# Transposing q, k and the attention output with the DMA crossbar instead of TensorE, in batches 3 to 7

## The chip, the cores and the metric

The kernel runs on one core of one Trainium2 chip. The metric is device time in microseconds (us); each kernel was run several times, and medians are quoted. The engines are called as the profile calls them: PE is TensorE (PEld its weight loads), DVE is VectorE, ACT is ScalarE, POOL is GpSimd, SP is SyncE. SP and POOL compute little here; POOL issues the loads, SP issues the stores and, after the change, the crossbar transposes. L508 in a profile line is line 508 of the kernel that the profile belongs to. In the rows of 40 digits each digit is the busy share of one of 40 equal slices of the span, in tenths (9 is 90% or more); PEclk is the clock granted to PE, in tenths of full speed. The line that begins with the shares of PE, DMA and so on ("PE 73%; DMA 10%") splits up the chain of waits that ended last. Of the tile names, duo and uno are PSUM tiles, the crossbar turns cb into qx and xb into xt, dl is the shift, xk and xr are the blends, rl and kk the mix before and after squaring, rs the sigmoid, ot the output.

## The reference

Eight batches of sliding-window attention with a linear position bias, then a channel mix, on 576 positions with 8 heads of 64.

```python
# attention: q, k, v are (8, 8, 576, 64)
scores = scale * np.matmul(q, k.transpose(0, 1, 3, 2))
mask = (rel >= 0) & (rel < 128)
scores = np.where(mask, scores + bias[None], -1000000000.0)
attn = softmax(scores)                      # written out in the reference
x = (attn @ v)                              # then heads side by side: (8, 576, 512)

# channel mix
x_prev = shift of x by one position, zeros first
xk = mu_k * x + (1.0 - mu_k) * x_prev
xr = mu_r * x + (1.0 - mu_r) * x_prev
k = np.maximum(xk @ w_k, 0.0)               # 512 -> 1024
v = k * k @ w_v                             # 1024 -> 512
r = 1.0 / (1.0 + np.exp(-(xr @ w_r)))
return r * v
```

Two transposes per batch follow from this. The scores need q and k with the head dimension on the partitions, while they are loaded with positions there. The mix needs the attention output with the model dimension on the partitions, while attention delivers it by positions.

## The kernel before

The kernel plans its own order. Each piece of work is a node with an engine, an assumed duration and latency, and a priority; a list scheduler written in Python plays the plan through once, at build time, and the order that it finds is the order in which every engine executes. On the chip the engines keep to this order: an instruction whose data are late holds up everything behind it on the same engine (a wait of 6.06 us is followed below). That matters for the whole argument.

```python
def rank(prio):                        # attention: due by its group, ahead of the mix by A
    ...
        return {e: ((k - A[e]) * 4.87,) + tuple(prio) for e in A}
...
A = {PE: 9.0, ACT: 7.0, DVE: 7.0, VIR: 0}
...
def full_load(b, i, h, g):             # q or k of one batch: 4 loads by POOL
    src = (q, k)[i][b, :, 0:SM].rearrange("h (p r) d -> p h r d", p=128)
    return [dma(POOL, 256, issue_t(1024), lambda e, r=r: nc.gpsimd.dma_start(
        out=cb_buf[h.idx][:, i, r], in_=src[:, :, r]), [g]) for r in range(NF)]
...
for g in range(G):                     # four groups of two heads in each batch
    ...
    def emit_t(e, g=g, hp=hp, hc=hc):
        for n in range(2 * NF):        # eight 128x128 transposes of q and k on PE
            nc.tensor.transpose(
                one(hp).bitcast(BF16)[:, 128 * n:128 * n + 128],
                cb_buf[hc.idx][:, n // NF, n % NF, 2 * g:2 * g + 2].rearrange(
                    "p h d -> p (h d)"), ident)
    t = op(PE, 0.0565 * 8, cl[b] + paced(b, g), prio + (3,), emit_t, [hp, hq], [hc])
    y = op(ACT, act_t(1024), [t], ...)             # copy out of PSUM
    _, (m0, m1) = scores(b, g, ...)
    r, hx = attend(b, g, 0, NJ, ha, [m0, m1] + vl[b], prio)   # PE, then DVE normalizes
    a, c = out_t(b, g, 0, NJ, hx, [r], prio, xh[P], xth[b])   # 5 PE transposes, ACT copy,
                                                              # DVE shift and two blends
...
# channel_mix ends each block of 128 rows with a store by SP, out of one of three buffers
y = plan.add(SPE, 0.6, 0.0, [d], (1, len(plan.nodes)),
             lambda e, ho=ho, row=row: nc.sync.dma_start(
    out=of[row:row + 128, :], in_=ot_buf[ho.idx]))
```

The softmax here doesn't subtract the row's maximum and nothing guards it: scores larger than these inputs give would overflow.

## Time and profile before

| | before |
|---|---|
| time, median of 4 runs | 254.72 us (253.82 to 255.14) |
| span of the profiled execution | 252.6 us |
| span less PE's busy time | 252.6 - 233.2 = 19.4 us |
| loads land within the first | about 161 us |

### The profile page before, as it was taken

What the parts mean: (1) busy time and instruction counts of PE and PEld (TensorE: products, weight loads), DVE (VectorE), ACT (ScalarE), POOL (GpSimd) and SP (SyncE); (2) the same over time, 40 slices, a digit from 0 to 9 for tenths busy, and PEclk for the clock granted to TensorE, in tenths of its full rate; (3) what the DMA queues carried; (4) which work ended last, traced back from release to release, by engine and by line L of the source; (5) the groups of instructions that cost most, each with busy time, mean ns of one, the idle gap of its engine ahead of it and who ended that gap; (6) DMA issues with size and microseconds to landing.
All of it is one profiled execution on the core that took longest, in us unless ns stands there. A gap on an engine that the chain in (4) does not pass through costs nothing.

```text
span 252.6 us, 5776 instructions
## 1 busy us (share of the span) xinstructions
PE 233.2 (92%) x2259; PEld 143.9 (57%) x2288; DVE 195.0 (77%) x433; ACT 175.3 (69%) x285; POOL 104.7 (41%) x130
## 2 busy tenths in 40 slices
PE   2979985989989999999999999999999999999993
PEld 1436764565655766556565775565666754445461
DVE  7676776789998999979995997897798887325242
ACT  3486889388896887888497795975896755426250
POOL 8959894899966580509540576000000000000000
PEclk9999999999999999999999999999999999999999
DMA  8999999999998997909991599902101202031112
GB/s 110 151 169 162 156 146 177 152 190 156 203 154 63 169 166 81 134 2 107 188 157 42 76 169 120 91 0 86 66 20 43 86 0 84 3 125 42 65 62 84
DMA packets 119916, 26.87 MB, mean 106 GB/s; under 512 B 112208, under 2 KB 114768, under 8 KB 119888
## 3 DMA queue, kind: packets, MB, share of 16 engines
q0 software_dynamic: 112560, 16.52, 95.2%
q1 hardware_dynamic: 7328, 9.97, 11.5%
q8 instruction: 18, 0.29, 0.5%
q14 instruction: 10, 0.08, 0.1%
HBM read 33.56 MB, written 9.44 MB: 170 GB/s over the span
## 4 chain that ended last, share of the span: by engine, by line
PE 73%; DMA 10%; DVE 5%; ACT 4%; issue 4%; POOL 2%; DVEq 0%; POOLq 0%; ACTq 0%
PE uno L628 23%; PE uno L661 21%; PE uno L647 10%; PE duo L485 5%; PE duo L525 5%; DMA wv_sb<-in_moe_w_v_dram 4%; PE uno L554 3%; PE uno L781 3%; ACT at L496 2%; DMA cb<-in_k_dram 2%; DMA ts<-in_k_dram 2%; PE duo L472 2%; POOL cb L365 2%; DMA out_dram<-ot 1%; PE uno L724 1%
## 5 line engine op out<-in xcount | busy, mean ns | idle before, releaser
L628 PE MATMUL uno<-xk,wk_sb 128*128 128x256 bf16 (+2 forms) x411 | 72.4, 318 | 1.1 <-DVE xk L573 0.8
L661 PE MATMUL uno<-wv_sb,kk 128*128 128x512 bf16 x280 | 70.5, 379 | 3.1 <-DMA wv_sb<-in_moe_w_v_dram 1.3
L496 ACT ACTIVATE at<-duo 128x1024 bf16<-128x1024 f32 (+2 forms) x68 | 65.5, 994 | 7.1 <-PE duo L485 6.8
L635 ACT ACTIVATE rl<-uno 128x256 bf16<-128x256 f32 (+2 forms) x104 | 47.8, 480 | 29.8 <-PE uno L628 26.9
L628 PEld LDWEIGHTS <-wk_sb 128*128 128x128 bf16 x416 | 39.1, 99 | 21.8 <-issue 1.3
L639 DVE TENSOR_TENSOR kk<-rl 128x256 bf16<-128x256 bf16 (+2 forms) x104 | 33.1, 338 | 13.1 <-ACT rl L635 11.8
L661 PEld LDWEIGHTS <-kk 128*128 128x128 bf16 x288 | 25.9, 98 | 28.2 <-DMA wv_sb<-in_moe_w_v_dram 1.4
L502 DVE TENSOR_TENSOR at<-at,mask 128x1024 bf16<-128x1024 bf16 x56 | 37.2, 684 | 4.9 <-ACT at L496 4.9
L672 DVE SCALAR_TENSOR_TENSOR ot<-rs,uno 128x512 f32<-128x512 bf16 x36 | 24.6, 683 | 18.3 <-PE uno L661 14.8
L455 ACT COPY qk<-uno 128x1024 bf16<-128x1024 bf16 (+1 forms) x30 | 30.1, 1004 | 10.3 <-PE uno L781 9.0
L344 POOL DMA_DIRECT2D vs<-in_v_dram x32 | 28.5, 902 | 19.8 <-PE duo L525 16.4
L647 PE MATMUL uno<-wr_sb,xr 128*128 128x512 bf16 x128 | 35.1, 379 | 0.9 <-issue 0.2
L365 POOL DMA_DIRECT2D cb<-in_q_dram x28 | 24.7, 904 | 24.8 <-PE uno L781 24.8
L654 ACT ACTIVATE rs<-uno 128x512 bf16<-128x512 f32 x36 | 22.0, 611 | 16.5 <-PE uno L647 14.2
L573 DVE SCALAR_TENSOR_TENSOR xk<-dl,muk_sb,xt 128x576 bf16<-128x576 bf16 (+2 forms) x36 | 26.9, 747 | 0.5
L365 POOL DMA_DIRECT2D cb<-in_k_dram x28 | 24.8, 914 | 6.0 <-DMA wv_sb<-in_moe_w_v_dram 4.2
L573 DVE SCALAR_TENSOR_TENSOR xr<-dl,mur_sb,xt 128x576 bf16<-128x576 bf16 (+2 forms) x36 | 26.8, 744 | 0.0
L525 PEld LDWEIGHTS <-at 128*128 128x128 bf16 x576 | 22.1, 99 | 6.9 <-ACT at L496 1.9
L455 ACT COPY xt<-uno 128x576 bf16<-128x576 bf16 (+2 forms) x36 | 21.2, 589 | 5.6 <-PE uno L554 4.8
L532 DVE TENSOR_TENSOR xu<-duo,rc 128x640 bf16<-128x640 f32 x28 | 23.1, 824 | 1.0
L647 PEld LDWEIGHTS <-xr 128*128 128x128 bf16 x144 | 13.7, 98 | 14.0 <-issue 0.2
L485 PE MATMUL duo<-qk 64*128 64x256 bf16 (+1 forms) x264 | 20.2, 262 | 1.2 <-DVE xu L532 1.2
(52 smaller groups left out, 215.1 us busy)
## 6 DMA issues: line engine op xcount, KB each, us to landing
out_dram<-ot SPq DMA_DIRECT2D x36, 256.0 KB, 2.1
vs<-in_v_dram POOLq DMA_DIRECT2D x32, 128.0 KB, 5.5
cb<-in_q_dram POOLq DMA_DIRECT2D x28, 128.0 KB, 6.4
cb<-in_k_dram POOLq DMA_DIRECT2D x28, 128.0 KB, 6.0
wk_sb<-in_moe_w_k_dram POOLq DMA_DIRECT2D x1, 1024.0 KB, 9.0
wv_sb<-in_moe_w_v_dram POOLq DMA_DIRECT2D x1, 1024.0 KB, 11.2
ts<-in_q_dram POOLq DMA_DIRECT2D x8, 64.0 KB, 5.7
ts<-in_k_dram POOLq DMA_DIRECT2D x8, 64.0 KB, 5.5
```

Source lines behind the costliest of these rows:

```text
L365: return [dma(POOL, 256, issue_t(1024), lambda e, r=r: nc.gpsimd.dma_start(out=cb_buf[h.idx][:, i, r], in_=src[:, :, r]), [g]) for r in ra ...
L455: (nc.scalar.copy if e == ACT else nc.vector.tensor_copy)(out=out, in_=in_)
L485: nc.tensor.matmul(sa[:, hl, c0:c0 + n], lhsT=kk_, rhs=qq_, start=not bias, stop=True, skip_group_check=True)
L496: lambda e, ah=ah, w=w, hp=hp: nc.scalar.activation(out=ah(), in_=two(hp)[:, :, 0:w], func=AF.Exp, scale=float(scale)), (), [hp])
L502: prio + (2,), lambda e, ah=ah, m0=m0, w=w: nc.vector.tensor_tensor(out=ah(), in0=ah(), in1=mask[:, 2 * g:2 * g + 2, m0:m0 + w], op=ALU.mu ...
L525: nc.tensor.matmul(a[:, hl, t - t0], lhsT=at[:, lo:lo + 128], rhs=vs[:, u, 2 * g + hl, :] if u < NF else tvb[:, 2 * g + hl], start=(u == u ...
L573: lambda e, buf=buf, mu=mu: nc.vector.scalar_tensor_tensor(out=buf[hk.idx][:, g, e0 + c0:e0 + c1], in0=dl_buf[hd.idx][:, 0:n], scalar=mu[: ...
L628: nc.tensor.matmul(one(hp)[:, 0:n], lhsT=wk_sb[:, po, 128 * fo:128 * fo + 128], rhs=xk_buf[hx.idx][:, po, c0:c1], start=(po == 0), stop=(p ...
L635: a = op(ACT, act_t(n), [s], pr, lambda e, hp=hp, hr=hr: nc.scalar.activation(out=rl_buf[hr.idx][:, 0:n], in_=one(hp)[:, 0:n], func=AF.Rel ...
L639: lambda e, fo=fo, hr=hr: nc.vector.tensor_tensor(out=kk_buf[hk.idx][:, fo, 0:n], in0=rl_buf[hr.idx][:, 0:n], in1=rl_buf[hr.idx][:, 0:n], ...
L647: nc.tensor.matmul(one(hp), lhsT=xr_buf[hx.idx][:, po, 128 * c:128 * c + 128], rhs=wr_sb[:, po], start=(po == 0), stop=(po == NPO - 1))
L661: nc.tensor.matmul(one(hv), lhsT=kk_buf[hk.idx][:, fo, o:o + 128], rhs=wv_sb[:, fo], start=(fo == 0), stop=(fo == NFO - 1))
```

## The change

The intent is to take transposes off PE, the busiest engine. From batch 3 on, one crossbar transpose turns a 128x512 block of q or k (all heads at once, eight per batch), straight from SBUF into SBUF, and five turn the attention output of a batch. PE's transposes and ACT's copies out of PSUM disappear there. The normalization may go to ACT or DVE, from batch 1 on. The shift and the two blends move to the end of each batch, and are ranked XD = 4 groups later. One PSUM buffer moves to the pool that mix and transposes now share, and the sigmoid buffers go from 6 to 4. Each load of q or k for these batches now brings 128 consecutive positions instead of every fourth one.

```diff
+    XB = range(3, B)          # batches whose q and k are turned by the crossbar
+    XO = range(3, B)          # batches whose attention output is
+    XD = 4
+    def XU(b, g):             # engines allowed for the normalization
+        return (ACT, DVE) if b else (DVE,)
...
+    qx_buf = many(2, [128, 2, G, SM], BF16, "qx")
+    xb_buf = many(2, [128, NJ, H, D], BF16, "xb")
-    rs_buf = many(6, [128, DM], BF16, "rs")
+    rs_buf = many(4, [128, DM], BF16, "rs")
-    N1 = 3
+    N1 = 4
+    PT = "p1"
...
+    def flip(b, i, j, g):     # one of eight for q and k of a batch
+        return dma(SPE, 190, 1.25, lambda e: nc.sync.dma_start_transpose(
+            out=qx_buf[xbh[b].idx][:, i, :, 128 * j:128 * j + 128],
+            in_=cb_buf[ch[b].idx][:, i, j].rearrange("p h d -> p (h d)")),
+            [g, (cl[b][NF * i + j], 6.0)], (), [ch[b]])
...
+            for t in range(nt):                       # normalization on ACT
+                for hl in range(2):
+                    nc.scalar.activation(out=out_[:, hl, t], in_=a5()[:, hl, t, 0:D],
+                                         func=AF.Copy, scale=rc[:, hl, t:t + 1])
...
+    def out_flip(b, rs, hx, ht):                      # five for the output of a batch
+        for t in range(NJ):
+            rows = min(128, S - 128 * t)
+            n = plan.add(SPE, 1.25 * rows / 128, 0.0, rs + [virt_xt[b]], ...
+                         nc.sync.dma_start_transpose(
+                out=xt_buf[ht.idx][:, :, X0 + 128 * t:X0 + 128 * t + rows],
+                in_=xb_buf[hx.idx][0:rows, t].rearrange("p h d -> p (h d)")))
+            res.append(plan.add(FAB, 0.6 * rows / 128, 0.9, [(n, 1.0)], ...))
...
+        if b in XO:
+            fl = out_flip(b, rs, xbh_o[b], xth[b])
+            for g in range(G):
+                xks[b, g], xrs[b, g] = shift(b, g, 0, S, fl, (0, b, 0, g + XD), xh[P], xth[b])
```

(Cut to its core; "..." marks the cuts, and comments are added.)

## The prediction

> **What bounds the kernel now.** I read three views of the profile in this order: the page of the execution (shares, slices, chain of waits), the busy time of each engine in stretches of the span, and the timeline of PE around single attention groups.
>
> ```profile
> PE 233.2 (92%) x2259; PEld 143.9 (57%) x2288; DVE 195.0 (77%) x433; ACT 175.3 (69%) x285; POOL 104.7 (41%) x130
> PE   2979985989989999999999999999999999999993
> DVE  7676776789998999979995997897798887325242
> ACT  3486889388896887888497795975896755426250
> DMA  8999999999998997909991599902101202031112
> PE 73%; DMA 10%; DVE 5%; ACT 4%; issue 4%; POOL 2%; DVEq 0%; POOLq 0%; ACTq 0%
> 75.00:210.00 135.00, 132.50 (x1361) 83.74 (x1380) 118.43 (x240) 103.31 (x162) 41.95 (x50) 1.00 0.86 90
> 210.00:248.50 38.50, 38.19 (x198) 19.45 (x200) 16.24 (x37) 16.85 (x33) 0.00 (x0) 1.00 0.15 57
> ```
>
> The last two lines give the stretch, its length, then busy us of PE, PEld, DVE, ACT and POOL (with instruction counts), the granted clock, the DMA share and GB/s. There are three stages. Up to about 75 us, PE has gaps and the chain of waits runs through loads: batches 1 to 3 come in as fast as the DMA brings them. From 75 to 210 us PE is busy 132.5 of 135 us, and attention (which runs ahead) and the channel mix share it. DVE is the runner-up at 118.43/135 = 88%, ACT has 77%. From 210 us on there is channel mix alone, PE at 99%, all others under half. So PE sets the end, and DVE stands close behind it in exactly the stage that the change touches. The granted clock is 1.00 throughout.
>
> **What the Trainium skill says.** (1) "Trainium Kernel Development and Optimization", Performance Expectations, calls matmul busy time a bad metric, because matmuls are pipelined. This trace agrees: eight transposes of q and k show 0.61 us and 219 ns each, so they start (0.61 - 0.22)/7 = 56 ns apart.
>
> ```profile
> 162.49 0.61 PE L781 MATMUL uno<-ident,cb 128*128 128x128 bf16 x8
> 162.94 1.89 PE L628 MATMUL uno<-xk,wk_sb 128*128 128x512 bf16 x8
> 164.66 0.44 PE L554 MATMUL uno<-ident,xu 128*128 128x128 bf16 x5
> 164.94 0.62 PE L525 MATMUL duo<-vs,at 128*128 128x65 bf16 x15
> ```
>
> Columns: start, us, engine, line, operation, count. The next matmul starts 0.45 us after the first of the eight, and 0.28 us after the first of the five transposes of the attention output. Those start-to-start times, not 0.61 and 0.44, are what a removal gives back on a full PE. (2) "VectorE: DVE Perf Modes", The three transpose paths: a 128x128 bf16 transpose takes 390 ns on TensorE and 1309 ns through the DMA crossbar, which leaves SBUF in SBUF while TensorE's lands in PSUM. The trace has 219 ns for TensorE, not 390, and no crossbar transpose yet; the PSUM copies it saves are in the trace. (3) "DMA: Bandwidth & Descriptors", Latency and other measured facts, gives 261 GB/s for a DMA transpose: as an estimate from that, 131 KB (128x512 bf16) is 0.50 us of all DMA engines. No run shows it yet. (4) The same page, Queues, rings and completion order: each DMA engine takes turns between queue rows packet by packet, so transposes from SP share with the loads from POOL. The output stores, which share in the same way, land in 2.1 us by the page, so that is tolerable today.
>
> **The change part by part**, for the 5 batches 3 to 7, 4 groups each, 20 groups.
>
> Removed from PE: per group 8 transposes of q and k and 5 of the output, 0.45 + 0.28 = 0.73 us; times 20 = **14.6 us** of PE issue. By busy time it would be 20 x (0.61 + 0.44) = 21 us, but the pipeline tails in that lie under the next matmul, so I do not count them.
>
> Removed from ACT: one copy of 128x1024 and one of 128x576 per group.
>
> ```profile
> L455 ACT COPY qk<-uno 128x1024 bf16<-128x1024 bf16 x28 | 29.0, 1034 | 9.2 <-PE uno L781 9.0
> L455 ACT COPY xt<-uno 128x576 bf16<-128x576 bf16 x28 | 18.0, 643 | 4.6 <-PE uno L554 4.6
> L532 DVE TENSOR_TENSOR xu<-duo,rc 128x640 bf16<-128x640 f32 x28 | 23.1, 824 | 1.0
> L654 ACT ACTIVATE rs<-uno 128x512 bf16<-128x512 f32 x36 | 22.0, 611 | 16.5 <-PE uno L647 14.2
> L496 ACT ACTIVATE at<-duo 128x1024 bf16<-128x1024 f32 x56 | 56.7, 1049 | 1.0 <-PE duo L485 0.9
> ```
>
> That is 20 x (1.03 + 0.64) = 33 us off ACT, all in the middle stage, none of it on the path by itself.
>
> Moved: the normalization (824 ns on DVE) may now go to ACT as ten 128x64 activations. The two ACT rows of 512 and 1024 columns give (1049 - 611)/512 = 0.86 ns a column and a fixed 170 ns, so one takes about 225 ns alone, and perhaps 100 to 200 ns in a row since neighbours overlap: an estimate of 1 to 2 us a group. If half of the 20 groups go there, DVE loses 10 x 0.82 = 8 us and ACT gains about 15. ACT ends near 103 - 33 + 15 = 85 us. The reciprocal, the shift and the two blends stay on DVE, but after the last group of a batch, as one burst of about 4 x (0.45 + 0.81 + 0.81) = 8.3 us.
>
> Does DVE hold the gain back? If the middle stage shrinks by 14.6 us to about 120 us, DVE has 118.4 - 8.2 = 110 us to do in it: 92%. With no move it would be 98%. So the move is what makes the gain possible, and at 92% I expect a little to be lost to queueing: 2 us.
>
> Added: 8 crossbar transposes per batch for q and k and 5 for the output, 65 in all, on SP's queue. The trace shows 21 groups of attention between 75 and 210 us, 6.4 us a group, 26 us a batch. The planner inside the kernel assumes 1.25 us of SP per transpose; taking that as the author's measurement, a batch costs 12.5 x 1.25 = 16 us of SP (the last output piece is half), inside the 23 us a batch has afterwards. The DMA share shows that transfers leave room after 100 us. Attention's result is needed late: by the last two stretches, mix goes on 40 us after attention has ended, so 8 us more from attention to mix is hidden. Loads have room as well: q and k now pass through two load buffers and two transposed ones, which is deeper than before.
>
> One place is exposed: batch 3. Its k loads land near 64 us and the first PE transposes wait for them, one buffer at a time:
>
> ```profile
> 63.51 0.55 PE L781 MATMUL uno<-ident,cb 128*128 128x128 bf16 x7
> 64.32 0.23 PE L781 MATMUL uno<-ident,cb 128*128 128x128 bf16 x1 [0.26 <-DMA cb<-in_k_dram]
> ```
>
> Now all eight crossbar transposes must land first, some 3 to 5 us after the last load (an estimate: two issues and a landing like that of the stores). PE has mix work meanwhile, so I count 1 us. In exchange, PE loses some small waits on ACT's copies and the mix gets a fourth PSUM bank: minus 0.5 us.
>
> **Sum**: 254.9 - 14.6 + 2 + 1 - 0.5 = 242.8; I say 243.0 us, 4.7% faster.
>
> **The rivals.** (a) *The crossbar becomes the bound.* The budget is about 23 us for 13 transposes, so about 1.8 us each. If one occupies the queue for 2.5 us, a batch needs 31 us, more than today's 26, and the kernel is slower, 258 to 275 us. For it: the 1309 ns for a quarter of such a transfer, and DMA slices at 9 up to 100 us. Against it: the 261 GB/s and the author's 1.25 us. (b) *DVE takes over* in the middle stage: if ACT gets few of the normalizations or the bursts collide with the squares for the mix, DVE runs at 98% and the gain halves, about 248 us. For it: DVE's row of nines today. (c) *SP's order turns into a wait*: SP runs in order, and a transpose that waits for a late load holds back the output stores behind it; three output buffers then stop DVE and PE. SP today only waits for outputs, so this is new; it could eat 3 to 10 us, giving 246 to 252. (d) *The gain is larger*, since PE today loses about 9% of the middle stage to small stalls that partly come from transposes waiting for ACT and DVE: at best the 21 us of busy time, 234 us.
>
> **Range and chances.** (b), (c) and a mild (a) pull up and (d) pulls down, so the range is lopsided: 235.0 to 253.0. The 2% line for faster is 249.8. I give (a) in full 0.12, (c) or (a) eating nearly all of the gain 0.15, the rest is faster: 0.73.
>
> **What would show it.** PE busy should fall to about 213 us, with no rows of transposes after batch 2 and the matmul counts 260 lower; ACT busy to about 157 us; the row of the normalization on DVE to about half its count; attention steps of about 5.7 us a group; PE still at nines to the end and still over 70% of the chain of waits. Issue to landing of the crossbar transposes should be 2 to 4 us. I am wrong if transposes or waits of SP stand in the chain, if DVE is at 97% between 75 and 200 us with gaps on PE beside it, if the stores land later and outputs wait for them, or if the tail of pure mix is longer than today's 40 us.

## More of the kernel before

The queue lines give packets, MB, and the time that the packets took as a share of 16 DMA engines over the whole span; the issue lines give count, KB each and the median us from issue to landing.

```profile
q0 software_dynamic: 112560, 16.52, 95.2%
q1 hardware_dynamic: 7328, 9.97, 11.5%
...
out_dram<-ot SPq DMA_DIRECT2D x36, 256.0 KB, 2.1
...
cb<-in_q_dram POOLq DMA_DIRECT2D x28, 128.0 KB, 6.4
```

Queue q0 holds POOL's loads, q1 what SP issues. The 95.2% are a share of the whole span, but the loads are over after some 161 us of it. While they run, their packets therefore take 95.2% x 252.6 / 161 = 149% of the engines' time: on average more than one packet is outstanding on every engine. This is time outstanding, not time occupied: the loads come in bursts. Counted from the packets of the trace between 60 and 160 us, none at all is in flight for 21.9 of the 100 us. That is the room that there is.

## The result, and the profile after

The changed kernel took 267.01 us, median of 4 runs (266.41 to 267.3), against 254.72: a ratio of 1.0485, interval 1.0451 to 1.0518. It is slower. All ratios here are the mean time of one kernel's fast runs over that of the other's fast runs of the same rounds, so they are not quite the ratio of the quoted medians.

From the page of the changed kernel: busy times, three rows of slices, the DMA queues and the chain that ended last.

```profile
PE 226.1 (85%) x2001; PEld 130.5 (49%) x2028; DVE 178.4 (67%) x412; ACT 184.5 (69%) x437; POOL 104.2 (39%) x130
PE   2879976989898689991898969997988999999994
PEclk9968999999999979998599979999999999999999
DMA  9999999999999999999999999997234112322122
...
q0 software_dynamic: 112560, 16.52, 105.2%
q1 hardware_dynamic: 41408, 18.17, 36.9%
...
PE 39%; DMA 21%; ACT 18%; DVE 11%; POOL 5%; issue 4%; DVEq 0%; POOLq 0%
```

The transposes have gone from PE (2259 matmuls before, 2001 now, 260 fewer by the program, since a trace can miss a few records), and PE is 7 us less busy. But the span is 265.5 us, so span less busy has grown from 19.4 to 39.4 us. PE's slices have holes in the middle stage, and in three places the granted clock drops beside them (a 7, then 8 and 5, then a 7, in slices 14, 18 to 19 and 23, counted from 0). The 6 and 8 in slices 2 and 3 are a drop at 15.4 us, before any crossbar transpose; the rows of few_loads and none_dummy have a shorter one there. DMA now stands at nines up to about 180 us, where it had gaps from 95 us on. PE's part of the chain fell from 73% to 39%; DMA has 21%.

The packets tell what a transpose is. Queue q1 went from 7328 to 41408 packets. The trace lists 32000 new ones of 256 bytes; with 60 full transposes and five of half size, that is 512 for each full one. They took 31.6 ns each on the mean, so the packets of one transpose take 512 x 31.6 / 16 = 1.01 us on each of the 16 DMA engines. A packet's time runs from its start to its end, also while others are in flight on its engine. When the loads are over (196 to 228 us), a packet of a transpose takes 17.8 ns: 0.57 us per engine, and a whole transpose is through within 0.63 us. So it is the company of the loads that makes it 1.01 us. It slows the loads too: their 128-byte packets take 38.2 ns instead of 32.6. The transposes that start before 160 us (40, counted in full ones) need 40 x 0.57 = 23 us even at the pace they have alone, as much as the room that there was; between 60 and 160 us there is now no moment without a packet in flight, and 1.97 are in flight per engine on the mean, where it was 1.43.

Next the groups of instructions that the change made (count | busy us, mean ns of one | idle time before, and what ended it), and the DMA issues, from the page and the view of the DMA queues.

```profile
L571 ACT ACTIVATE xb<-duo,rc 128x64 bf16<-128x64 f32 x160 | 34.8, 359 | 16.4 <-DVE rc L560 16.4
L613 DVE TENSOR_TENSOR dl<-xt 128x576 bf16<-128x576 bf16 (+2 forms) x36 | 14.8, 421 | 14.6 <-DMA xt<-xb 11.8
out_dram<-ot SPq DMA_DIRECT2D x36, 256.0 KB, 3.4
cb<-in_q_dram POOLq DMA_DIRECT2D x28, 128.0 KB, 10.7
qx<-cb SPq DMA_TRANSPOSE x40, 7.8
xt<-xb SPq DMA_TRANSPOSE x25, 6.7
```

A transpose lands 6.7 to 7.8 us after its issue. The loads of q now take 10.7 us instead of 6.4, and the stores 3.4 instead of 2.1. Sixteen of the 20 groups are normalized on ACT (160 activations, ten a group). DVE waits 11.8 us in all for the transposed output (tile xt, in the row of dl).

One such wait, followed to its end. First the timeline of the changed kernel (start, us, engine, line, operation, count, and in brackets the idle time before it with what ended it), then its busy times in stretches (the columns as in the prediction).

```profile
120.59 0.83 DVE L613 TENSOR_TENSOR dl<-xt 128x576 bf16<-128x576 bf16 x2 [6.06 <-DMA xt<-xb]
...
124.37 2.16 ACT L571 ACTIVATE xb<-duo,rc 128x64 bf16<-128x64 f32 x10 [6.16 <-DVE rc L560]
...
126.58 0.51 PE L508 MATMUL duo<-qx 64*128 64x256 bf16 x4 [6.09 <-ACT xb L571]
```

```profile
115.00:120.00 5.00, 4.89 (x39) 2.28 (x36) 0.00 (x0) 2.10 (x7) 1.59 (x3) 1.00 2.03 104
120.00:125.00 5.00, 0.49 (x5) 0.21 (x5) 4.41 (x9) 0.63 (x4) 2.34 (x4) 0.97 1.65 149
125.00:130.00 5.00, 3.20 (x17) 1.73 (x18) 4.88 (x8) 3.85 (x11) 2.12 (x3) 0.50 1.87 180
```

The five output transposes of batch 3 were issued from 105.2 to 110.7 us; the last landed at 120.4, 9.65 us after its issue. DVE's next instruction in its fixed order is the shift that needs it, so DVE does nothing for 6.06 us (0.00 in the first stretch). The reciprocal of the next attention group lies behind the shift on DVE; ACT waits 6.16 us for it with its ten activations; PE waits 6.09 us for the PSUM tile that those free. And when PE comes back at 126.58, its granted clock is 0.50, and stays there until 131.5. "TensorE: Matmul & The Clock Gate", section Why this matters for your kernels, in the Trainium skill advises no PE-idle gaps above about 3 us; this trace agrees, with 6.09 us idle and then the clock at one half. Two shorter gaps, 2.09 us until 94.0 and 2.43 us until 154.8, are also followed by 3.4 us at one half.

### The profile page after: what moved, and what is told of

Its sections match the earlier page's. It is cut to its first block, busy times and chain, and to the rows that moved or that the text cites. A ratio compares the mean times of both kernels' runs of the same rounds, so it can differ in the third digit from the quotient of the medians.

```text
span 265.5 us, 5512 instructions
## 1 busy us (share of the span) xinstructions
PE 226.1 (85%) x2001; PEld 130.5 (49%) x2028; DVE 178.4 (67%) x412; ACT 184.5 (69%) x437; POOL 104.2 (39%) x130
## 3 DMA queue, kind: packets, MB, share of 16 engines
q0 software_dynamic: 112560, 16.52, 105.2%
q1 hardware_dynamic: 41408, 18.17, 36.9%
## 4 chain that ended last, share of the span: by engine, by line
PE 39%; DMA 21%; ACT 18%; DVE 11%; POOL 5%; issue 4%; DVEq 0%; POOLq 0%
PE uno L720 13%; PE uno L687 12%; ACT xb L571 8%; DMA xt<-xb 8%; PE uno L706 6%; DMA ts<-in_k_dram 6%; DMA wv_sb<-in_moe_w_v_dram 4%; ACT rl L694 4%; ACT at L519 4%; PE duo L508 3%; DVE at L525 3%; DMA out_dram<-ot 2%; POOL qx L353 2%; DVE xk L619 2%; DVE ot L731 2%
## 5 line engine op out<-in xcount | busy, mean ns | idle before, releaser
L720 PE MATMUL uno<-wv_sb,kk 128*128 128x512 bf16 x274 | 72.2, 389 | 3.3 <-DMA wv_sb<-in_moe_w_v_dram 1.8
L519 ACT ACTIVATE at<-duo 128x1024 bf16<-128x1024 f32 (+2 forms) x68 | 66.3, 1013 | 9.3 <-PE duo L508 9.0
L687 PEld LDWEIGHTS <-wk_sb 128*128 128x128 bf16 x416 | 40.3, 100 | 32.4 <-issue 9.6
L698 DVE TENSOR_TENSOR kk<-rl 128x256 bf16<-128x256 bf16 (+2 forms) x104 | 33.2, 337 | 21.9 <-ACT rl L694 20.7
L571 ACT ACTIVATE xb<-duo,rc 128x64 bf16<-128x64 f32 x160 | 34.8, 359 | 16.4 <-DVE rc L560 16.4
L720 PEld LDWEIGHTS <-kk 128*128 128x128 bf16 x288 | 26.6, 99 | 30.8 <-issue 1.9
L713 ACT ACTIVATE rs<-uno 128x512 bf16<-128x512 f32 x36 | 22.5, 631 | 22.5 <-PE uno L706 22.4
L706 PE MATMUL uno<-wr_sb,xr 128*128 128x512 bf16 x135 | 37.2, 386 | 0.7 <-issue 0.2
L554 PEld LDWEIGHTS <-at 128*128 128x128 bf16 x576 | 21.9, 98 | 9.8 <-ACT at L519 1.9
L613 DVE TENSOR_TENSOR dl<-xt 128x576 bf16<-128x576 bf16 (+2 forms) x36 | 14.8, 421 | 14.6 <-DMA xt<-xb 11.8
L508 PE MATMUL duo<-qx 64*128 64x256 bf16 (+1 forms) x160 | 13.1, 274 | 9.5 <-ACT xb L571 8.5
L554 PE MATMUL duo<-vs,at 128*128 128x65 bf16 x448 | 19.6, 194 | 1.8 <-DVE at L525 0.8
L706 PEld LDWEIGHTS <-xr 128*128 128x128 bf16 x144 | 13.6, 100 | 14.7 <-issue 1.8
## 6 DMA issues: line engine op xcount, KB each, us to landing
cb<-in_q_dram POOLq DMA_DIRECT2D x28, 128.0 KB, 10.7
```

Source lines behind the costliest of these rows:

```text
L519: lambda e, ah=ah, w=w, hp=hp: nc.scalar.activation(out=ah(), in_=two(hp)[:, :, 0:w], func=AF.Exp, scale=float(scale)), (), [hp])
L554: nc.tensor.matmul(a[:, hl, t - t0], lhsT=at[:, lo:lo + 128], rhs=vs[:, u, 2 * g + hl, :] if u < NF else tvb[:, 2 * g + hl], start=(u == u ...
L571: nc.scalar.activation(out=out_[:, hl, t], in_=a5()[:, hl, t, 0:D], func=AF.Copy, scale=rc[:, hl, t:t + 1])
L687: nc.tensor.matmul(one(hp)[:, 0:n], lhsT=wk_sb[:, po, 128 * fo:128 * fo + 128], rhs=xk_buf[hx.idx][:, po, c0:c1], start=(po == 0), stop=(p ...
L698: lambda e, fo=fo, hr=hr: nc.vector.tensor_tensor(out=kk_buf[hk.idx][:, fo, 0:n], in0=rl_buf[hr.idx][:, 0:n], in1=rl_buf[hr.idx][:, 0:n], ...
L706: nc.tensor.matmul(one(hp), lhsT=xr_buf[hx.idx][:, po, 128 * c:128 * c + 128], rhs=wr_sb[:, po], start=(po == 0), stop=(po == NPO - 1))
```

## The experiments

Theory T, formed on this result and the first runs below: the saving on PE is real, but the 65 transposes share the DMA engines with the loads; loads, stores and transposes all land later, and in the fixed order each late landing runs through DVE and ACT to PE. The expectations below use the letters of their time: A is an earlier form of T, in which DVE's wait for the output transposes is the loss; A2 is T; B says that the transposes of q and k crowd the loads, C that the normalization on ACT costs (R3); H says that the order has used up the lead of attention over the mix. Rivals: R1, one of the two transposes is to blame by its place in the order (output stores behind transposes on SP, or the output's way to the mix); R2, the plan believes in too short a landing and could be put right; R3, the loss comes from the other parts of the change (normalization on ACT, buffers), not from the crossbar.

### One transpose alone: qk_only and out_only

```diff
# qk_only                          # out_only
-    XO = range(3, B)              -    XB = range(3, B)
+    XO = range(B, B)              +    XB = range(B, B)
```

> Crossbar for q and k alone; the attention output goes back to PE. Theory A (the changed kernel is slow because its output transposes land 7 to 10 us after issue, and VectorE, which works in a fixed order, stands still at the first subtraction of a batch, up to 6 us at a time): the waits of VectorE for the output transposes, 11.8 us in total, are gone, PE has no hole at 120 to 130 us, the granted clock is back at 0.98 or more, and the time falls to 245 to 256 us. Rival B (the q and k transposes crowd the loads, whose landing went from 6 to 11 us, so attention starves): stays at 260 us or above, with landing of the q and k loads still about 10 us. Rival C (ten small ScalarE normalizations a group hold up the exponentials): stays above 260 us, since they are still there.

> Crossbar for the attention output alone; q and k go back to PE. Theory A: remains slow, above 260 us if the landing of the output transposes stays above 6 us; but if the landing falls to about 2.4 us wherever no loads run, part of the loss goes, 255 to 260 us. Rival B (the q and k transposes crowd the loads): time falls to 250 us or below and the loads land in 6 us again.

Measured: qk_only 264.57 us, ratio 1.0385 (1.0322 to 1.0447); out_only 262.09 us, ratio 1.0287 (1.02 to 1.0373). Both halves cost time, so neither is the culprit alone. (In their rounds the kernel before took 255.19 us, in those of the change 254.72, so differences of under 1 us mean little.) The expectation that qk_only would be at 245 to 256 us if the output's way were the path was missed. In qk_only the effect that rival (c) of the prediction named appears. The waits (us in total, times, longest) and the timeline of that kernel:

```profile
DVE ot L731 <- DMA out_dram<-ot: 13.6, 4, 5.6
134.23 0.69 DVE L731 SCALAR_TENSOR_TENSOR ot<-rs,uno 128x512 f32<-128x512 bf16 x1 [5.59 <-DMA out_dram<-ot]
134.97 0.81 PE L687 MATMUL uno<-xk,wk_sb 128*128 128x384 bf16 x4 [2.52 <-DVE ot L731]
```

DVE waits for an output buffer whose store is late, and PE waits for DVE. The cause that (c) gave, SP's order, is only a part of it: SP issued this store 1.62 us after its data were ready, and then it took 6.73 us to land.

### More output buffers: qk_only_ot6

If those buffers are the path, six instead of three must win time. The full change has no room for six (building it stops with a need of 211.9 KB in each partition where 207.9 are left), so the test was made on qk_only, without the unused xb buffers.

```diff
-    XO = range(3, B)
+    XO = range(B, B)
-    ot_buf = many(3, [128, DM], FP32, "ot")
+    ot_buf = many(6, [128, DM], FP32, "ot")      # and ot=6 in the plan; xb_buf dropped
```

> The run with q and k alone on the crossbar, with six output buffers instead of three (the room comes from the unused buffer of the attention output). Theory A2 with the order of SP as its path: VectorE's wait of 13.6 us for output stores, which stand behind transposes that wait for late loads, falls under 3 us, and the time falls from 264.6 by 6 us or more, to 250 to 258 us. If the output stores are not the path: 262 us or above.

Measured: 264.78 us, ratio 1.0422 (1.0374 to 1.0469), the same as qk_only. The wait for stores fell from 13.6 to 8.3 us, and no time was won. So 5.3 us of this wait could go without gain. The expectation asked for a wait under 3 us, and that was not reached, so the test makes the buffers unlikely as the cause and does not exclude them.

### The plan told the truth, or reordered: told_late, xd0, lead13

The plan believed that an output transpose lands 0.9 us after its transfer. Told_late raises that by 5 us. Xd0 takes back the four-group delay of shift and blends. Lead13 lets attention run four groups further ahead of the mix.

```diff
# told_late
-            res.append(plan.add(FAB, 0.6 * rows / 128, 0.9, [(n, 1.0)], ...
+            res.append(plan.add(FAB, 0.6 * rows / 128, 5.9, [(n, 1.0)], ...
# xd0
-    XD = 4
+    XD = 0
# lead13
-    A = {PE: 9.0, ACT: 7.0, DVE: 7.0, VIR: 0}
+    A = {PE: 13.0, ACT: 11.0, DVE: 11.0, VIR: 0}
```

> The changed kernel with one number of its planner changed: it is told that an output transpose lands 5 us later than it believed (0.6 + 5.9 us instead of 0.6 + 0.9 after the issue), so it places the subtractions later in VectorE's fixed order. Same instructions, same transfers. Theory A: VectorE's waits for the output transposes fall from 11.8 us to under 3 us, the hole of PE at 120 to 130 us goes, clock 0.98 or more, time 250 to 258 us. Rivals B and C: nothing changes by more than 3 us, 263 to 269 us.

> The changed kernel with the shift and blends of batches 3 to 7 given the rank of their own group instead of four groups later (one number in the planner). Theory H (the gathering of a whole batch, the transposes' landing and the late rank together use up the lead of attention over the mix: from batch 3 on, the mix of a batch starts 1 to 5 us after its last blend, where it had 14 to 26 us before): the last blends of batches 3 to 7 end 5 to 10 us sooner after the batch's last attention, and the time falls by 5 us or more, to 262 us or less. Theory A (VectorE stands at the first subtraction until the transposes land): the subtractions now stand earlier in its order, so its waits for output transposes grow from 11.8 us to 20 us or more and the time stays at 265 to 275 us.

> The changed kernel with attention ranked four groups further ahead of the mix (one line of the planner). Theory H: if the order can win back a lead, the time falls by 4 us or more, to 263 us or less; if attention itself comes late because loads, transposes and ScalarE hold it, the rank changes nothing, 264 to 270 us.

Measured: told_late 275.03 us (ratio 1.0799), xd0 274.46 us (1.0759). Both are slower than the change itself. Of lead13's four runs three were slow; the one fast run took 270.34 us, no gain either. Told_late carries a warning about the wait followed above: DVE's wait for the output transposes did fall as intended, from 11.8 to 0.5 us, but the time rose by 8 us instead of falling, and PE still has a hole of 5.09 us at 125 us. So that one wait is an instance of the loss, not its source. From the waits of xd0 (us in total, times, longest):

```profile
PE uno L706 <- ACT rl L694: 10.7, 1, 10.7
ACT rl L694 <- DVE kk L698: 10.6, 2, 10.4
```

Placed earlier, the twelve shifts and blends of a batch stand as one block, with their wait for the transposes, in front of the squares that the mix needs; PE then stands 10.7 us in one piece. Placed later, the mix starves. So R2 is not borne out: none of the three orders tried repairs it. That does not prove that no order could.

### Other parts of the change: none, none_dve, norm_dve

None turns both crossbar transposes off and keeps the normalization's choice, the PSUM pool and the buffers (the late shift and the new order of the loads go with the transposes); none_dve also leaves the normalization on DVE; norm_dve is the whole change with the normalization on DVE.

```diff
# none                             # none_dve: none, and      # norm_dve: only
-    XB = range(3, B)              -  return (ACT, DVE) if b else (DVE,)
+    XB = range(B, B)              +  return (DVE,)
-    XO = range(3, B)
+    XO = range(B, B)
```

> The changed kernel with no crossbar transpose at all: PE transposes everything as before; what is left of the change is the normalization on ScalarE or VectorE from batch 1 on, four PSUM banks in one pool, four instead of six sigmoid buffers. Theory A2: within 2% of the kernel before, 250 to 259 us. Rival C (normalization on ScalarE costs): 258 to 264 us, as slow as the runs with one of the two transposes.

> The same with all normalization on VectorE: what is left is the PSUM pool and the buffers. All theories: within 2% of the kernel before, 251 to 258 us; if it is slower by more, the buffers have a share in the loss.

> The changed kernel with all normalization on VectorE. Rival C (the small ScalarE activations, 2.1 us for ten where VectorE needs 0.82 us): the time falls by 8 us or more, to 259 us or below, and ScalarE's busy time falls by about 35 us. Theory A: the wait for the output transposes is untouched, so 262 to 270 us.

Measured: none 259.69 us, ratio 1.0211 (1.0153 to 1.0269); none_dve 256.71 us, 1.011 (1.0031 to 1.0188); norm_dve 272.98 us, 1.0699 (1.0615 to 1.0782). So R3 is right in part. Before any transpose moves, what none_dve keeps (the buffer split and the normalization as two separate steps) costs about 1%, and the normalization on ACT about another 3.0 us (256.71 to 259.69; the two sets of four runs just touch). Both crossbar transposes then add 267.01 - 259.69 = 7.3 us; q and k alone add 4.9, the output alone 2.4, the same sum within the noise. With the transposes on the crossbar, the sign for the normalization turns: on DVE the kernel is 6 us slower than with ACT's help.

### Fewer loads: few_loads and none_few

This is the main test. From batch 3 on, only two of eight heads of q, k and v are loaded, with the same number of DMA instructions (queue q0 has 66480 packets instead of 112560). The result is wrong (relative error 0.76 for few_loads), while the compute engines have the same work. If T holds, the crossbar now gains; if the crossbar is slow for itself, the loss stays.

```diff
+        nh = 2 if b >= 3 else H
-            out=cb_buf[h.idx][:, i, r], in_=src[:, :, r]), [g]) for r in range(NF)]
+            out=cb_buf[h.idx][:, i, r, 0:nh], in_=src[:, 0:nh, r]), [g]) for r in range(NF)]
# v in the same way; few_loads is the change with this, none_few is none with this
```

> The changed kernel, but from batch 3 on only two of eight heads of q, k and v are loaded, so the result is wrong on purpose (stale data stands in the other heads); all engine work and all 65 transposes stay. Theory A2 (transposes and loads contend on the 16 DMA engines, and the late landings stop engines that work in a fixed order): transposes land in 2.3 to 4 us instead of 6.7 to 7.8 us, no hole in PE, clock above 0.98, time 240 to 250 us. Rival C (the normalization on ScalarE) and a rival in which the transposes themselves are too slow on SP's queue at 1.25 us each: 260 us or above.

> The run without crossbar transposes (259.7 us) with two of eight heads loaded from batch 3 on (wrong on purpose). It is the control of the run with few loads (248.7 us). If lighter loads help only because transposes and loads contend, this gains little: 256 to 260 us. If it falls to 250 us or less, the loads slow the kernel without any crossbar transposes, and the run with few loads says little about contention.

| median us (ratio to before) | all loads | a quarter of q, k, v from batch 3 on |
|---|---|---|
| transposes on PE | none: 259.69 (1.0211) | none_few: 258.2 (1.0159) |
| transposes on the crossbar | the change: 267.01 (1.0485) | few_loads: 248.74 (0.9785) |

With all loads the crossbar costs 7.3 us; with a quarter of them it gains 9.5 us. The smaller loads by themselves, with transposes on PE, are worth 1.5 us only. The loss is therefore an interaction of transposes and loads. The packets agree: between 60 and 160 us few_loads has 22.5 us with none in flight, the change 0.0. The page and the DMA view of few_loads:

```profile
PE 220.7 (89%) x2001; PEld 128.8 (52%) x2028; DVE 178.5 (72%) x412; ACT 183.1 (74%) x437; POOL 93.8 (38%) x130
...
PE 50%; ACT 24%; DVE 11%; DMA 5%; POOL 4%; issue 4%; DVEq 0%; POOLq 0%; ACTq 0%
...
qx<-cb SPq DMA_TRANSPOSE x40, 4.0
...
xt<-xb SPq DMA_TRANSPOSE x25, 2.9
```

The same transposes land in 4.0 and 2.9 us instead of 7.8 and 6.7, their 256-byte packets take 22.3 ns instead of 31.6, and DMA has 5% of the chain instead of 21%. Set against none_few (span 255.6 us, PE busy 233.6), PE is 12.9 us less busy and idle 4.7 us more (247.4 - 220.7 = 26.7, against 22.0). In the changed kernel, set against none (span 258.0, busy 233.9), PE is 7.8 us less busy but idle 15.3 us more (39.4 against 24.1). Part of the smaller saving is the clock: its mean is 0.96 in the changed kernel and 0.984 in few_loads, and the 128x512 matmuls on w_v take 389 ns on the mean instead of 379.

### Few loads and no delay: few_xd0

```diff
-    XD = 4
+    XD = 0        # with the loads of few_loads; wrong result on purpose
```

> As the run with few loads (248.7 us, wrong on purpose), and the blends with the rank of their own group. With the contention taken away, theory H says that the lead comes back: mix of batches 4 to 7 starts 5 us or more after the last blend, and the time falls to 240 to 245 us, near what the removed PE work is worth. If 248 us or more, the late rank was not what was left.

Measured: 261.0 us, ratio 1.0216 (1.0126 to 1.0306), both of the three fast runs (with the slow one the median is 261.5). Even with little on the DMA, the block of shifts and blends in its early place costs 12.3 us against few_loads. The delay XD = 4 is right for this kernel; that contention takes away what it leaves is the reading of few_loads.

### Transposes that nobody needs: none_dummy and none_dummy_wait

The opposite test: PE keeps all of its transposes, and 65 crossbar transposes are added that read a constant tile into unused buffers. In none_dummy_wait, those for q and k read the real loads, so that SP must wait for these.

```diff
# none, and:
+            if b >= 3:
+                for i in range(2):
+                    for j in range(NF):
+                        dma(SPE, 190, 1.25, lambda e, i=i, j=j, b=b: nc.sync.dma_start_transpose(
+                            out=qx_buf[b % 2][:, i, :, 128 * j:128 * j + 128], in_=wk_sb[:, 0, 0:512]),
+                            [(cl[b][NF * i + j], 6.0)], (), ())
# five more at the end of each batch's attention, in_=wk_sb[0:rows, 0, 0:512]
# none_dummy_wait: in_=cb_buf[ch[b].idx][:, i, j] for q and k
```

> The run without crossbar transposes (259.7 us; PE transposes everything) plus the same 65 crossbar transposes as dummies: they read a resident weight, write unused buffers, and nothing waits for them. If contention on the DMA engines is itself the loss: 264 us or above, loads landing in 9 us or more instead of 6. If the loss comes from engines that wait for the transposes' results: 258 to 262 us although the dummies land late.

> As the run with dummies, but the 40 q and k dummies read the real load buffers, so SP waits for the loads, output stores stand behind them in its order, and a load buffer is held until its dummies have read it. Nothing waits for their results. If SP's order matters: 3 us or more above the run with plain dummies, with waits of VectorE for output stores of 5 us or more. If not: within 2 us of it.

Measured: none_dummy 266.65 us, ratio 1.0511 (1.0444 to 1.0578), which is 7.0 us more than none; none_dummy_wait 265.78 us, 1.045 (1.0399 to 1.05), no worse. The presence of the transposes on SP's queue and on the DMA engines costs 7 us, with no data of theirs waited for. In none_dummy the loads of q land in 9.0 us (6.1 in none) and the stores in 3.0 (2.0). The loads keep their old order in these runs, so the new one is not needed for the loss. The starts of the mix's blocks show where it happens: 128, 148 and 160 us in none, 130, 154 and 166 in none_dummy, and after that the distance stays at 7. One wait and two entries of the timeline of none_dummy, then a stretch of its busy times:

```profile
DVE ot L737 <- DMA out_dram<-ot: 8.0, 4, 3.6
134.66 0.69 DVE L737 SCALAR_TENSOR_TENSOR ot<-rs,uno 128x512 f32<-128x512 bf16 x1 [3.63 <-DMA out_dram<-ot]
135.40 2.34 PE L693 MATMUL uno<-xk,wk_sb 128*128 128x384 bf16 x8 [2.70 <-DVE ot L737]
135.00:140.00 5.00, 4.61 (x39) 3.25 (x39) 4.39 (x11) 3.29 (x5) 0.83 (x1) 0.66 1.71 164
```

A store is late, DVE waits 3.63 us for its buffer, PE 2.70 us for DVE, and the clock in the next 5 us is 0.66 on the mean. SP had issued this store 0.03 us after its data were ready; it took 5.7 us to land. So here it is not SP's order that makes it late.

### Stores taken off SP: none_dummy_act and stores_act

To part SP's order from the shared DMA engines, the stores were issued by ACT.

```diff
-                         lambda e, ho=ho, row=row: nc.sync.dma_start(
+                         lambda e, ho=ho, row=row: nc.scalar.dma_start(
# none_dummy_act: none_dummy with this; stores_act: the change with this
```

> The run with dummies, with the 36 output stores issued from ScalarE's queue instead of SP's. If the stores' place behind the transposes in SP's queue is the path: VectorE's wait of 8.0 us for stores falls under 3 us, the hole of PE near 132 us and the granted clock of 0.66 after it go, and the time falls by 4 us or more, to 262 us or less. If the shared DMA engines are the path whatever the queue: 264 us or above.

> The changed kernel with the output stores issued from ScalarE's queue. The wait of VectorE for stores (4.4 us) goes, but its wait for the output transposes (11.8 us) stays, so I expect 262 to 267 us; under 255 us would make it the better kernel.

Measured: none_dummy_act 323.95 us (ratio 1.2739), stores_act 281.17 us (1.1058). The first says nothing on the question. Without the stores between them the dummies ran from 16 us on, and ACT stood 45.8 us before one store, by the trace until the landing of a dummy. In stores_act, ACT waits 17.0 us before two stores, by the trace for transposes of q and k. A store on ACT's queue brings a new in-order wait on a busy engine here; in the trace of stores_act, six of the 36 stores wait for a semaphore that transposes on SP raise too. So this test could not part the two. The traces of none and none_dummy go further: of the stores between 60 and 185 us, SP issued each 0.19 us on the mean after its data were ready in none_dummy (at most 1.1) and 0.03 in none, while landing took 5.9 us on the mean instead of 3.5. In none_dummy the stores are late in the transfer and hardly in SP's order. How much of the 7 us comes through late stores and how much through late loads stays open.

### Only where loads are rarer: late67

Crossbar for q and k of batches 6 and 7 and for the output of batch 7 only, with normalization, delay and PSUM split as before.

```diff
-    XB = range(3, B)
-    XO = range(3, B)
+    XB = (6, 7)
+    XO = (7,)
# XD = 0, XU returns (DVE,), N1 = 3, PT = "pt"
```

> A version meant to win: crossbar for q and k of batches 6 and 7 and the output of batch 7 only, when few or no loads are under way; normalization on VectorE, own PSUM bank for transposes as before, blends at their own rank. PE loses 8 x 0.45 + 4 x 0.28 = 4.7 us of issue. Theories H and A2: transposes land in 2.3 to 4 us, no new holes, 249 to 254 us. If crossbar transposes cost even without loads beside them: 256 us or above.

Measured: 257.99 us, ratio 1.0131 (1.0072 to 1.0191), both of its three fast runs (258.42 with the slow one). It is not slower by over 2%, and nothing is won. The expectation read 256 us or above as a cost of the transposes without loads; but none_dve, with no transposes, is as far off (1.011), so this run does not show such a cost. No run beat the kernel before with a correct result; the nearest is none_dve at 256.71 us, so the kernel before stays the one to use.

## Why the prediction was wrong

It said 243.0 us, 235 to 253, and faster; 267.01 us was measured.

- **What bounds the kernel**: right. PE is the engine to relieve, as few_loads showed: the crossbar wins 9.5 us there.
- **14.6 us of PE removed**: the counting was right (2001 matmuls instead of 2259) and the saving exists. Against none_few, few_loads has PE busy 12.9 us less. The 213 us that I named as a sign mixed this up with the 20 us of busy time that I had just refused to count; 226.1 was measured, and 220.7 with a quarter of the loads.
- **"The DMA share shows that transfers leave room after 100 us"**: this is the step that failed. I read room off the slices of one row after 100 us, where a nine is a ceiling, and did not read the queue table. There was room, but not enough: no packet in flight for 21.9 us between 60 and 160, against 23 us for the transposes that start in that time, and 0.0 us were left. The term "0.50 us of all DMA engines" was not the fault: alone a transpose takes 0.57 us. Wrong was to use it as if it were alone; beside the loads its packets take 1.01 us. And "issue to landing 2 to 4 us" became 6.7 and 7.8; it was 4.0 and 2.9 in few_loads. The sum had no term for what 65 transposes do to loads and stores. It measures 7.0 us in none_dummy, with PE's work untouched.
- **1.25 us of SP for a transpose**: right, 1.2 to 1.3 us in most of the trace. The budget of SP was not the limit.
- **"8 us more from attention to mix is hidden"**: too small and not hidden. From the last reciprocal of a batch to the end of its last blend it took 5 to 8 us before and 18 to 29 after (batches 3 to 7). Their blends for xk were ready 14 to 24 us ahead of their mix block before, and 1 to 6 after. In few_loads that lead is as short, 1 to 6 us, and the kernel is fast. So the plan has spent its slack on the delay, which alone does no harm, but a late landing then goes straight through to PE.
- **Batch 3 exposed, +1 us**: wrong in the harmless direction. Its transposes landed up to 17 us after the last load, not 3 to 5, and its first scores still began at 82.1 us, against 82.4 in none. That the plan had no earlier place for them on PE would explain it; it was not tested.
- **Half of the normalizations on ACT, 1 to 2 us each**: 16 of the 20 groups went there, at 34.8 / 16 = 2.2 us, and three more of batches 1 and 2. So ACT is at 175.3 - 33.4 + 19 x 2.2 = 184 us, as measured (184.5), and not at 157. DVE fell by 16.6 us instead of 8. One activation alone was estimated at 225 ns and took 359; the estimate of ten in a row, 1 to 2 us, came near the 2.2. The plan believed 0.105 us an activation, half of what ten in a row take each; that it chose ACT too often for this reason was not tested. I took this part as a help for DVE; without the crossbar it costs 3.0 us.
- **Gain from "a fourth PSUM bank", -0.5 us**: not seen. With the sigmoid buffers cut to four and the normalization in two steps it comes to a loss of about 1% (none_dve).
- **The rivals**: (a) had the right range, 258 to 275 us, with the wrong mechanism: the queue is not occupied for 2.5 us by a transpose, the DMA engines are shared. That its range fits is luck. I gave it 0.12. The end of (c), DVE and PE standing for a late store, is visible in qk_only and none_dummy, but its cause, SP's order, is a small part there (1.62 us and 0.03 us for the two stores followed), and six output buffers did not win anything. It is one of several ways by which late transfers reach PE. (b), DVE as the bound, did not occur: DVE is less busy and stands waiting. (d) rested on a wrong reading: PE does not lose 9% of the middle stage to stalls, its own line has it busy 132.50 of 135 us.
- **The signs of being wrong**: two came true. Transposes stand in the chain (DMA xt<-xb has 8% of it), and stores land later (3.4 us instead of 2.1) with outputs waiting for them.

## What to carry to other kernels

Before work is moved from an engine to the DMA, read the time of each queue's packets over the stretch in which that queue is active, not over the span, and for how much of it nothing is in flight; set the engines' time of all new transfers against that, and expect each packet to take longer in company; the loads that it delays belong in the sum. In a kernel whose engines keep a fixed order, a transfer's landing time is as good as its slack, so ask for the lead that the plan leaves, and what stands behind the first instruction that waits. A test with smaller loads and one with added transfers that nobody needs show, each beside its control, whether contention is the matter.

## What the Trainium skill lacked or had wrong

- "DMA: Bandwidth & Descriptors", Latency and other measured facts: the 261 GB/s for a DMA transpose led to an estimate of 0.50 us for 128x512 bf16. Alone it took 0.57 us of all 16 engines here (512 packets of 256 bytes at 17.8 ns), so the figure is near. That section gives none for transposes next to other traffic: beside the loads the packets took 31.6 ns (1.01 us), beside a quarter of them 22.3 ns (0.71 us). From issue to landing it was 2.3 us with the loads over, and up to 10 us beside them.
- "Advanced Engine Details and Errata", X-Bar Transpose (TRN2), says that transpose DMAs are as fast as regular ones. Here, with nothing else in flight, a transpose of 131 KB took 0.63 us from its first packet to its last (208 GB/s), a store of 262 KB on the same queue 0.79 us (332 GB/s). The packets are not alike, 256 bytes against 2048.
- "VectorE: DVE Perf Modes", The three transpose paths: 390 ns for TensorE, where the trace shows 219 ns for one and 56 ns between starts in a row. The second is what a removal saves.
- "TensorE: Matmul & The Clock Gate", Why this matters for your kernels: the advice to avoid gaps above about 3 us held at 6.09 us, but gaps of 2.09 and 2.43 us (the changed kernel) and 2.70 us (none_dummy) were also followed by 3.4 us at half the clock. One of 2.70 us in out_only, at 33 us, was not.
